# Sums of x in a two-layer kernel: their places in the passes moved, the first groups loaded ahead, the second layer's first buffers swapped

## The chip, the cores and the metric

The kernel runs on one core of one Trainium2 chip. The metric is device time in microseconds (us), the median of several executions. Three executions of the kernel before took 1288.52, 1289.45 and 1290.34 us. TensorE (PE) multiplies, its weight loads (PEld) run beside it; ScalarE (ACT), VectorE (DVE) and GpSimd (POOL) work element by element, and SyncE (SP) hands out nearly all DMAs, in the order in which they stand on its queue.

## The reference, cut to what matters

```python
# attention: q, k, v of (8, 8, 576, 64)
scores = scale * np.matmul(q, k.transpose(0, 1, 3, 2))
thresh = np.max(scores, axis=-1, keepdims=True) - tau
scores = np.where(scores >= thresh, scores, -1e9)
attn = softmax(scores)                      # written out in the reference
attn_out = np.matmul(attn, v)
x = attn_out.transpose(0, 2, 1, 3).reshape(4608, 512)
# two layers
h = np.maximum(x @ w_in, 0.0)               # (4608, 512) @ (512, 2048)
out = h * h @ w_out                         # (4608, 2048) @ (2048, 512)
```

All of it is float32. The change concerns the two layers after the attention.

## The kernel before, in words

**Stages.** The attention writes x transposed to DRAM (`xT`, one tensor for each of the 8 batches). The first layer begins at 496 us of the profiled execution and goes to 889 us, the second from there to the end. Both are multiplied by a scheme of Strassen's kind, applied twice (an outer and an inner level): instead of 8 x 8 = 64 block products it makes 7 x 7 = 49, and pays for that with sums of blocks ahead of the products and behind them. The seven operands of a level are called 1 to 7. Four of them (1, 7, 2, 3 for x) are the blocks themselves; 5, 6, 4 and a new 7 are sums: `SUMS_B` says 5 = 7 - 1, 6 = 3 - 5, 4 = 2 - 6, 7 = 3 - 7, in this order, the last one in place.

**Passes and products.** The first layer has nine passes, 0 to 8 (`PASSES`). They work on six sets of x (`SETS`), of 512 or 1024 columns: set 0 in pass 0, set 1 in passes 1 and 2, set 2 in 3 and 4, set 3 in 5 and 6, set 4 in pass 7 and set 5 in pass 8. Each of the two passes of a wide set has half of the outputs. A pass has 49 products, 0 to 48: seven groups, one for each outer operand m in the order 1, 2, 6, 7, 4, 5, 3 (`OUTER`), and in each group seven products for the inner operands in the order 1, 6, 7, 5, 2, 4, 3. A product fills one PSUM bank of 512 columns. A wide product is two matmuls of 256 columns, a narrow one four of 128; in the trace each matmul leaves two records.

**A group** (`inner`, L729 to L761) uses four banks, X, Y, Z, W, of six in a ring. X is copied to SBUF by ACT (`p1`, L764), Y and Z are taken out by DVE with a sum (`u2`, `u3`, L128), W by DVE with a sum; then three more products are added into X, Z and W, each of which needs the bank to have been read, and are taken out as well. In group 1 the last X is a copy by ACT (L951). `final` (L947) adds the results up, on DVE where nothing else is added and else as a DVE sum into a ring of six places `t` and a POOL addition (L128 on POOL) that reads the place. Groups 2, 4, 5 and 3 give outputs `o`.

**Squares.** Each output is squared by ACT in two instructions (`square`, L905 and L906) and stored by SP (L909). `squares_due(6)` at the end of each product's `tick` takes one from the list when it is five products old. So the squares of group 3, made in products 45 to 48, stand on ACT's queue in products 1 to 4 of the next pass, behind those of group 5 (products 43 to 46).

**Sums of x.** While two passes run on one set, the sums of the next set are made by ACT and DVE together: `sum_v` (L855) lets ACT copy one operand to a PSUM place `c` (L868; two such places) and returns the DVE operation that subtracts it (L125). `plan` (L1189) says for each set what is loaded and summed at which product, counted from the beginning of two passes: `loads` issue DMAs from `xT` (`load_set`, L828), `work` makes sums. `sum_outer` makes a whole outer operand from raw ones, in chunk 0 (inner 1 and 7) or 1 (inner 2 and 3); `sum_inner` makes one inner operand for one or more outer ones at once, if their places lie at even distances. The copy of a sum is issued at its product, and `finish_sum` (L1197), called at every product, issues the DVE operation at the next one. The places of the sets in SBUF (`PLACES`, `AT[4]`) are chosen so that a group of the next set comes into a place that a group of the set before has left; a load waits for that.

**Beside these** POOL makes sums of the second layer's weights in small steps (`chain_out`, L1168): SP loads four blocks from DRAM (L1180), POOL makes four subtractions (L125 on POOL), SP stores the results (L1185). In pass 7 the sums of set 5 are made by `prepare_x`, one step at a product (L1254). In the last pass the first sums for the second layer are made.

**The second layer** (`output_layer`, L1043) has nine passes of narrow products (L1074) on the stored squares. It has the same groups; its places come from rings `fin` (L994 to L998), among them `t` for p1, u2 and u3. At each product `also` (L1287) does part of the list of sums (`work_of`, `spread`) and, while any is left from the first layer, a square. Place 13 * 512, the first of ring `t`, is the last of the four places that pass 8 keeps for U2 and that POOL reads at its end.

The order of all of this is written out by hand (`manual_schedule`): each engine's queue holds its instructions in the order in which the program issues them.

## Time and profile before

| what | value |
|---|---|
| median of 3 executions | 1289.45 us |
| the profiled execution | 1290.65 us |
| its span, first to last instruction | 1288.8 us |
| mean granted TensorE clock in it | 0.997 |
| first layer's products in the span | 496.2 to 889.0 us |
| second layer's products | from 889.1 us |

One execution is profiled. A row of a timeline has the start in us from the beginning of the span, the length in us, engine, line, operation, written and read names, sizes and the count of merged instructions; in brackets stands how long the engine stood idle before it and who ended that. A row of the groups or the issues has count and then mean or median; a row of the waits has total us, times and the longest. Lines are those of the kernel before.

### The profile page before, as it was taken

Reading aid. Unit: us, or ns where it says so; the run is one execution under the profiler, and the core shown is the slowest. Engines: PE = TensorE matmul, PEld = TensorE weight load, DVE = VectorE, ACT = ScalarE, POOL = GpSimd, SP = SyncE. Lnnn points to the kernel's source line nnn. Section 1 sums busy time; section 2 is a strip of 40 time slices with the busy share of each in tenths; the row PEclk is TensorE's granted clock in tenths of the full one; section 3 lists DMA queues with packets and bytes.
Section 4 is the critical chain, followed back from the end, with each engine's and each line's share of the span. In section 5 each row is a group of like instructions: output and inputs, shape, how many; then the busy total and the mean of one; then the engine's idle time right before and its main releaser. Section 6 shows DMA issues by size and latency. Waiting matters only on the chain. (4 is left out here: it accounts for less than half of the span.)

```text
span 1288.8 us, 44113 instructions
## 1 busy us (share of the span) xinstructions
PE 1259.3 (98%) x17451; PEld 1090.0 (85%) x17451; DVE 998.9 (78%) x2437; ACT 852.9 (66%) x1540; POOL 897.4 (70%) x1094
## 2 busy tenths in 40 slices
PE   8999999999999999999999999999999999999998
PEld 5666666677777769988888888999999999999998
DVE  6999999999999997887778777877745664665463
ACT  6999999999999994655765766666523432343240
POOL 2565656655555556887797788768777867776775
PEclk9999999999999999999999999999999999999999
DMA  5555666544333423457567556589545314522411
GB/s 143 147 160 145 164 195 189 142 95 112 90 81 88 101 46 99 158 160 218 181 196 213 175 180 190 184 316 393 193 147 164 109 61 160 164 80 89 160 34 34
DMA packets 256590, 191.88 MB, mean 149 GB/s; under 512 B 96000, under 2 KB 217344, under 8 KB 256384
## 3 DMA queue, kind: packets, MB, share of 16 engines
q1 hardware_dynamic: 254928, 188.63, 49.1%
q8 instruction: 137, 2.24, 0.7%
q14 instruction: 69, 0.57, 0.1%
q10 hardware_dynamic: 1456, 0.44, 0.1%
HBM read 116.65 MB, written 72.35 MB: 147 GB/s over the span
## 5 line engine op out<-in xcount | busy, mean ns | idle before, releaser
L128 POOL TENSOR_TENSOR arena<-arena 128x512 f32<-128x512 f32 (+1 forms) x314 | 377.9, 1222 | 130.3 <-DVE arena L128 117.3
L1074 PE MATMUL po<-wall,arena 128*128 128x128 f32 x3528 | 394.7, 275 | 1.4 <-ACT arena L764 1.4
L1074 PEld LDWEIGHTS po<-wall,arena 128*128 128x128 f32 x3528 | 394.2, 192 | 1.8 <-ACT arena L764 1.8
L935 PE MATMUL ph<-arena,wall 128*128 128x128 f32 (+1 forms) x2352 | 389.4, 328 | 4.1 <-DVE arena L128 3.3
L935 PEld LDWEIGHTS ph<-arena,wall 128*128 128x128 f32 x2352 | 353.8, 191 | 39.6 <-DVE arena L128 7.9
L128 DVE TENSOR_TENSOR arena<-ph,arena 128x512 f32<-128x512 f32 x378 | 253.8, 687 | 71.9 <-PE ph L935 43.5
L125 POOL TENSOR_TENSOR arena<-arena 128x128 f32<-128x128 f32 (+2 forms) x314 | 255.3, 814 | 31.8 <-DMA arena<-w 13.8
L128 DVE TENSOR_TENSOR arena<-po,arena 128x128 f32<-128x128 f32 x378 | 108.2, 289 | 168.7 <-PE po L1074 164.5
L469 ACT ACTIVATE arena<-arena 128x576 f32<-128x576 f32 x288 | 227.7, 885 | 16.2 <-DVE arena L459 16.2
L474 DVE SCALAR_TENSOR_TENSOR arena<-arena 128x576 f32<-128x576 f32 x288 | 225.6, 812 | 0.5 <-POOL arena L466 0.5
L459 DVE TENSOR_SCALAR_CACHE_REDUCE arena<-sc 128x576 f32<-128x576 f32 x288 | 204.4, 750 | 15.6 <-ACT arena L531 6.4
L868 ACT COPY c<-arena 128x512 f32<-128x512 f32 (+3 forms) x307 | 173.9, 573 | 62.7 <-DVE arena L125 54.1
L125 DVE TENSOR_TENSOR arena<-arena,c 128x512 f32<-128x512 f32 (+3 forms) x271 | 175.3, 655 | 18.6 <-ACT c L868 15.8
L540 PEld LDWEIGHTS sc<-arena 64*64 64x64 f32 x5760 | 146.0, 134 | 42.4 <-DVE arena L459 38.9
L441 PE MATMUL sc<-arena 64*64 64x64 f32 (+1 forms) x2304 | 170.9, 417 | 0.4 <-DVE arena L661 0.4
L540 PE MATMUL sc<-arena 64*64 64x128 f32 (+1 forms) x5760 | 162.1, 263 | 8.4 <-DVE arena L459 6.2
L531 ACT COPY arena<-pt 128x1024 f32<-128x1024 f32 x144 | 161.2, 1119 | 3.7 <-PE pt L384 3.7
L764 ACT COPY arena<-po 128x128 f32<-128x128 f32 x63 | 16.6, 264 | 186.8 <-PE po L1074 184.0
L384 PEld LDWEIGHTS pt<-ident,arena 64*128 64x128 f32 x2304 | 83.0, 139 | 43.1 <-ACT arena L531 36.0
L764 ACT COPY arena<-ph 128x512 f32<-128x512 f32 x63 | 36.6, 581 | 104.7 <-PE ph L935 104.6
L384 PE MATMUL pt<-ident,arena 64*128 64x64 f32 x2304 | 100.7, 227 | 4.0 <-ACT arena L531 3.8
L441 PEld LDWEIGHTS sc<-arena 64*64 64x64 f32 x2304 | 64.1, 133 | 47.0 <-issue 22.2
(51 smaller groups left out, 952.2 us busy)
## 6 DMA issues: line engine op xcount, KB each, us to landing
g<-arena SPq DMA_DIRECT2D x144, 256.0 KB, 2.6
arena<-g SPq DMA_DIRECT2D x144, 256.0 KB, 5.0
w<-arena SPq DMA_DIRECT2D x60, 256.0 KB, 2.5
wall<-w SPq DMA_DIRECT2D x49, 256.0 KB, 5.2
arena<-w SPq DMA_DIRECT2D x44, 256.0 KB, 3.4
arena<-in_v_dram SPq DMA_DIRECT2D x32, 288.0 KB, 3.8
out_dram<-arena SPq DMA_DIRECT2D x70, 128.0 KB, 2.2
arena<-in_q_dram SPq DMA_DIRECT2D x64, 128.0 KB, 4.0
```

The source lines that it names most:

```text
L125: e.tensor_tensor(out=out, in0=x, in1=y, op=ALU.subtract)
L128: e.tensor_tensor(out=out, in0=x, in1=y, op=ALU.add)
L384: made = nc.tensor.transpose(pt[:, r, ts(slot, HALF)], of[rows, :], ident[rows, rows])
L441: made = nc.tensor.matmul(sc[at, ds(to, count)], lhs, kT[rows, ds(at_k, count)], start=True, stop=True)
L459: made = nc.vector.tensor_scalar(out=s[:, j, :], in0=sc[:, ds(at, S)], scalar1=1.0, scalar2=None, op0=ALU.mult, op1=ALU.min, accum_out=nmx ...
L469: nc.scalar.activation(out=w[:, :, j, :], in_=of(j), func=AF.Exp, bias=nmx[:, j : j + 1], scale=-1.0)
L474: nc.vector.scalar_tensor_tensor(out=w[:, :, j, :], in0=of(j), scalar=thr[:, j : j + 1], in1=w[:, :, j, :], op0=ALU.is_le, op1=ALU.mult, a ...
L531: touch("weights", nc.scalar.copy(joined(to), whole(pt, 0, count)), at, 2 * BANK, m)
L540: made = nc.tensor.matmul(sc[ds(u * D, D), ds(5 * j * BANK + row, count)], loaded_v[i][rows, (c - (u != j)) % CH, :], wT[m][rows, ds(weigh ...
L868: nc.scalar.copy(c, y)
L935: nc.tensor.matmul(to[:, j, :], W_IN[m, k][:, ts(h * parts_ + j, P)], x_of(m, k), start=(not more and j == 0), stop=True, skip_group_check ...
L1074: nc.tensor.matmul(to, g[:, j, :], w[:, j, :], start=(not more and j == 0), stop=(j == 3), skip_group_check=True)
```

## The change

The change moves work and adds none to PE.

- `finish_sum` and `summed`: the DVE operation of a sum is issued two products behind its copy (or with the next sum's copy, if that comes earlier), not one.
- The plans of sets 1 to 4 are written anew. No sum stands in the last products of a pass or the first five of the next one; in between they stand closer, mostly two products apart. Inner sums of group 2 are made early and alone, those of 6 with 7 and of 4 with 5 in pairs, those of 3 alone.
- Loads: group 1 of sets 2 and 3 (and 1 and 7 of set 4) is loaded 14 products before the two passes begin. Group 2 is loaded at product 21 and group 3 at 28, where it was the other way round. Set 4's second load goes from product 14 to 7.
- `PLACES` and `AT[4]` follow from that. Inner operand 7 of group 2 is no longer made in place but at a place of its own (`ASIDE`), as outer sum 4 still reads the raw one later.
- Pass 7: the steps of `prepare_x` stand in products 17 to 40 without a pause, not in the first six of each seven from product 14.
- Second layer: the two halves of ring `t` change their order; the four outer sums of its first group are put ahead of the sum for inner operand 7 of group 2; what is left of the squares goes at the second and third product of a group, not at the last two.

```diff
@@ places
-        1: {7: 0, 1: 1, 2: 2, 3: 3, 5: 4, 6: 5, 4: 6},
-        2: {1: 7, 7: 1, 5: 2, 3: 5, 2: 0, 6: 6, 4: 4},
-        3: {1: 3, 7: 7, 5: 0, 3: 6, 2: 1, 6: 4, 4: 2},
+        1: {1: 0, 7: 1, 2: 2, 3: 3, 5: 4, 6: 5, 4: 6},
+        2: {1: 7, 7: 0, 5: 2, 2: 5, 3: 1, 6: 6, 4: 4},
+        3: {1: 3, 7: 7, 5: 5, 2: 6, 3: 0, 6: 4, 4: 2},
...
+        if w > NQ and (m, k) == (2, 7):
+            return arena[:, ds(ASIDE, w)]
@@ rings of the second layer
-    fin.ring("t", [13 * BANK + P * i for i in range(4)] + [XI + 2 * BANK + P * i for i in range(4)])
+    fin.ring("t", [XI + 2 * BANK + P * i for i in range(4)] + [13 * BANK + P * i for i in range(4)])
@@ the plans
-        def finish_sum():
-            while open_sum:
-                open_sum.popleft()()
+        def finish_sum(wait=2):
+            while open_sum and open_sum[0][0] + wait <= clock["n"]:
+                open_sum.popleft()[1]()
...
         tail = {
-            57: (out_, 4, 1), 60: (in_, (7, 4), 5), 63: (in_, (7, 4), 6), 66: (in_, (7, 4), 7), 69: (in_, (7, 4), 4),
-            72: (in_, (5, 3), 5), 75: (in_, (5, 3), 6), 78: (in_, (5, 3), 7), 81: (in_, (5, 3), 4),
+            54: (out_, 4, 0), 56: (in_, (6, 7), 5), 58: (in_, (6, 7), 6), 60: (in_, (6, 7), 7), 62: (in_, (6, 7), 4), 65: (out_, 4, 1),
+            68: (in_, (4, 5), 5), 70: (in_, (4, 5), 6), 72: (in_, (4, 5), 7), 74: (in_, (4, 5), 4),
+            78: (in_, (3,), 5), 81: (in_, (3,), 6), 83: (in_, (3,), 7), 85: (in_, (3,), 4),
         }
         plan(1, 0, {0: (7, 1, 3, 2)}, {
-            9: (out_, 5, 0), 12: (out_, 5, 1), 15: (in_, (1,), 5), 18: (in_, (1,), 6), 21: (in_, (1,), 4), 24: (out_, 6, 0),
-            27: (out_, 6, 1), 30: (out_, 7, 0), 33: (out_, 7, 1), 36: (in_, (1,), 7), 39: (out_, 4, 0),
-            42: (in_, (2, 6), 5), 45: (in_, (2, 6), 6), 48: (in_, (2, 6), 7), 52: (in_, (2, 6), 4), **tail,
+            10: (in_, (1,), 5), 12: (in_, (1,), 6), 14: (in_, (1,), 4), 16: (out_, 5, 0), 19: (out_, 5, 1), 21: (in_, (1,), 7),
+            23: (out_, 6, 0), 26: (out_, 6, 1), 29: (out_, 7, 0), 31: (out_, 7, 1),
+            34: (in_, (2,), 5), 36: (in_, (2,), 6), 38: (in_, (2,), 7), 40: (in_, (2,), 4), **tail,
         })
         for i in (2, 3):
-            plan(i, (2 * i - 2) * 49, {0: (1,), 7: (7,), 21: (3,), 28: (2,)}, {
-                6: (in_, (1,), 5), 9: (in_, (1,), 6), 12: (in_, (1,), 4), 15: (out_, 5, 0), 18: (out_, 5, 1), 21: (in_, (1,), 7),
-                27: (out_, 7, 0), 30: (out_, 7, 1), 36: (out_, 6, 0), 39: (out_, 6, 1), 43: (out_, 4, 0),
-                46: (in_, (2, 6), 5), 48: (in_, (2, 6), 6), 51: (in_, (2, 6), 7), 54: (in_, (2, 6), 4), **tail,
+            plan(i, (2 * i - 2) * 49, {-14: (1,), 7: (7,), 21: (2,), 28: (3,)}, {
+                8: (in_, (1,), 5), 10: (in_, (1,), 6), 12: (in_, (1,), 4), 15: (out_, 5, 0), 18: (out_, 5, 1), 21: (in_, (1,), 7),
+                27: (in_, (2,), 5), 29: (in_, (2,), 6), 31: (in_, (2,), 7), 33: (in_, (2,), 4),
+                35: (out_, 6, 0), 37: (out_, 7, 0), 39: (out_, 6, 1), 41: (out_, 7, 1), **tail,
             })
         four = (1, 7, 2, 3)
-        plan(4, 6 * 49, {7: (1, 7), 14: (3, 2)}, {
-            22: (out_, 5), 25: (out_, 7), 28: (in_, four, 5), 31: (in_, four, 6), 34: (in_, four, 4), 37: (out_, 6), 40: (out_, 4),
-            43: (in_, four, 7), 46: (in_, (6, 4), 5), 49: (in_, (6, 4), 6), 52: (in_, (6, 4), 7), 55: (in_, (6, 4), 4),
-            58: (in_, (5,), 5), 61: (in_, (5,), 6), 64: (in_, (5,), 7), 67: (in_, (5,), 4),
+        plan(4, 6 * 49, {-14: (1, 7), 7: (3, 2)}, {
+            22: (out_, 5), 24: (out_, 7), 27: (in_, four, 5), 29: (in_, four, 6), 31: (in_, four, 4), 35: (out_, 6), 38: (out_, 4),
+            41: (in_, four, 7), 54: (in_, (6, 4), 5), 56: (in_, (6, 4), 6), 58: (in_, (6, 4), 7), 60: (in_, (6, 4), 4),
+            62: (in_, (5,), 5), 63: (in_, (5,), 6), 64: (in_, (5,), 7), 65: (in_, (5,), 4),
         })
@@ pass 7, and the second layer's lists
-                if before_last and 2 <= i <= 5 and at < 6:
+                if before_last and 17 <= tick < 41:
                     next(xsums)
...
-                    work += outer_sums(0, 6, (1, 2)) + outer_sums(0, 5, (4,)) + outer_sums(0, 6, (4,))
+                    work[3:3] = outer_sums(0, 6, (1, 2)) + outer_sums(0, 5, (4,)) + outer_sums(0, 6, (4,))
...
-                if at > 4:
+                if at in (1, 2):
                     squares_due(0)
```

More of the change, by code (lines that the diff above doesn't have):

```diff
@@ L783 @@
     AT[4] = {}
-    for m, s_, e in ((1, 3, 0), (7, 3, 1), (2, 1, 0), (3, 1, 1), (5, 4, 0), (6, 2, 0), (4, 2, 1)):
+    for m, s_, e in ((1, 1, 0), (7, 1, 1), (2, 3, 0), (3, 3, 1), (5, 4, 0), (6, 2, 0), (4, 2, 1)):
         AT[4][m] = SPOT[s_] + GROUP * e
@@ L836, in sum_inner @@
         op, x, y = next((op, x, y) for op, z, x, y in SUMS_B if z == o)
+        if ms == (2,) and o == 7:
+            return add(op, x_block(i, 2, 7), x_blocks(i, ms, x), x_blocks(i, ms, y))
         return add(op, x_blocks(i, ms, o), x_blocks(i, ms, x), x_blocks(i, ms, y))
@@ L969, in final @@
                     row, col = {2: (0, 0), 4: (1, 0), 5: (1, 1), 3: (0, 1)}[m]
-                    squares.append((clock["n"], s, 4 * (2 * row + ab[0]) + 2 * col + ab[1], o))
+                    squares.append((clock["n"] , s, 4 * (2 * row + ab[0]) + 2 * col + ab[1], o))
             def tick(at):
```

9 lines of the change are left out of this document (5 added, 4 removed).

## The prediction

> **What bounds the kernel now.** I read the page first, then the timelines of PE and of its weight loads, then those of ACT, DVE, SP and POOL around the places where PE stops. Passes 0 to 8 are those of the first layer, products 0 to 48 the steps of a pass; a wide product is four records, a narrow one (passes 0, 7, 8 and the second layer) eight.
>
> ```profile
> span 1288.8 us, 44113 instructions
> PE 1259.3 (98%) x17451; PEld 1090.0 (85%) x17451; DVE 998.9 (78%) x2437; ACT 852.9 (66%) x1540; POOL 897.4 (70%) x1094
> ```
>
> PE is busy almost throughout; the change leaves its records as they are. It can only take away the moments in which PE waits. The timeline of PE merges records that follow each other and starts a new row where it waited:
>
> ```profile
> 593.90 36.53 PE L935 MATMUL ph<-arena,wall 128*128 128x256 f32 x168 [0.47 <-DVE arena L128]
> 630.75 6.52 PE L935 MATMUL ph<-arena,wall 128*128 128x256 f32 x28 [0.33 <-DVE arena L128]
> 637.77 79.30 PE L935 MATMUL ph<-arena,wall 128*128 128x256 f32 x364 [0.50 <-DVE arena L128]
> 717.56 6.52 PE L935 MATMUL ph<-arena,wall 128*128 128x256 f32 x28 [0.49 <-DVE arena L128]
> 724.58 79.74 PE L935 MATMUL ph<-arena,wall 128*128 128x256 f32 x384 [0.50 <-DVE arena L128]
> 805.07 6.52 PE L935 MATMUL ph<-arena,wall 128*128 128x128 f32 x56 [0.75 <-DVE arena L128]
> 811.88 18.39 PE L935 MATMUL ph<-arena,wall 128*128 128x128 f32 x160 [0.29 <-DVE arena L128]
> ...
> 889.07 3.74 PE L1074 MATMUL po<-wall,arena 128*128 128x128 f32 x32
> 893.36 12.83 PE L1074 MATMUL po<-wall,arena 128*128 128x128 f32 x112 [0.56 <-ACT arena L764]
> 907.05 378.14 PE L1074 MATMUL po<-wall,arena 128*128 128x128 f32 x3384 [0.86 <-ACT arena L764]
> ```
>
> The first record of the first layer stands in the view of its line, and the weight loads have a stretch without a wait:
>
> ```profile
> L935 PE MATMUL ph<-arena,wall x2352: 273/378/483, 496.2 to 889.0; 128*128 128x128 f32 x98, 128*128 128x256 f32 x98
> ```
> ```profile
> 645.04 70.66 PEld L935 LDWEIGHTS ph<-arena,wall 128*128 128x128 f32 x328 [0.16 <-DVE arena L128]
> ```
>
> 70.66/328 = 0.2154 us for a wide record, 378.14/3384 = 0.1117 for a narrow one; a wide product is 0.862 us, a narrow one 0.894. Counted out between the row starts, the lost time is:
>
> - start (496.2) to 593.90, product 12 of pass 2: 392 narrow and 244 wide records are 96.4 us, 97.65 passed: **1.3** lost.
> - to 637.77, product 12 of pass 3: 196 wide, 42.2 of 43.87: **1.65**.
> - to 724.58, product 12 of pass 5: 392 wide, 84.4 of 86.81: **2.4**.
> - to 811.88, product 12 of pass 7: 344 wide, 96 narrow, 84.8 of 87.30: **2.5**.
> - to 889.07: 688 narrow, 76.9 of 77.19: **0.3**.
> - the second layer to 907.05: 144 narrow, 16.1 of 17.98: **1.9**. From there on nothing.
>
> Together 10.0 us. That is all the change can win: it doesn't touch the attention part.
>
> The losses stand at the starts of passes 3, 5 and 7, and the reason is read on ACT and DVE at the start of pass 5:
>
> ```profile
> 713.60 0.63 ACT L905 ACTIVATE arena<-arena 128x512 f32<-128x512 f32 x1 [0.69 <-POOL arena L128]
> ...
> 714.79 0.58 ACT L868 COPY c<-arena 128x512 f32<-128x512 f32 x1
> ...
> 716.06 0.63 ACT L905 ACTIVATE arena<-arena 128x512 f32<-128x512 f32 x1 [0.17 <-POOL arena L128]
> ...
> 717.26 0.58 ACT L868 COPY c<-arena 128x512 f32<-128x512 f32 x1
> 717.77 0.62 ACT L905 ACTIVATE arena<-arena 128x512 f32<-128x512 f32 x1
> ...
> 720.14 0.57 ACT L951 COPY arena<-ph 128x512 f32<-128x512 f32 x1
> 720.61 0.63 ACT L905 ACTIVATE arena<-arena 128x512 f32<-128x512 f32 x1
> ...
> 721.81 0.58 ACT L868 COPY c<-arena 128x512 f32<-128x512 f32 x1
> 722.32 0.58 ACT L764 COPY arena<-ph 128x512 f32<-128x512 f32 x1
> ```
> ```profile
> 712.37 0.69 DVE L128 TENSOR_TENSOR arena<-ph,arena 128x512 f32<-128x512 f32 x1 [0.65 <-POOL arena L128]
> 712.97 0.68 DVE L125 TENSOR_TENSOR arena<-arena,c 128x512 f32<-128x512 f32 x1
> 714.83 0.69 DVE L128 TENSOR_TENSOR arena<-ph,arena 128x512 f32<-128x512 f32 x1 [1.17 <-POOL arena L128]
> ...
> 722.42 0.69 DVE L125 TENSOR_TENSOR arena<-arena,c 128x512 f32<-128x512 f32 x1 [2.13 <-ACT c L868]
> 723.02 1.51 DVE L128 TENSOR_TENSOR arena<-ph,arena 128x512 f32<-128x512 f32 x2
> ```
>
> ACT still has the squares of the pass before (L905 with L906, 1.2 us from start to start), some held by POOL, and copies for sums of x between them. So p1 of group 2 (L764, 722.32) is late, DVE waits 2.13 for a copy, and the eviction that frees product 12's bank (second of the two at 723.02) ends at 724.53: PE starts at 724.58.
>
> **The change part by part.**
>
> *No sums of x around a start, copies two products ahead* (L1187 to L1226). The built kernel's instruction order has no copy c from product 42 of a pass to product 4 of the next; the copy after the eight squares is at product 5, and p1 of group 2 stands behind it, as now. Of the copies above, that at 714.79 lies in the wait for POOL that ends at 716.06, so taking it away wins nothing; only the one at 717.26 stands on the path. Without it: square to 717.26, two more to 719.64, L951 to 720.11, the last square to 721.31, copy, p1 at 721.82 instead of 722.32: **0.5** at pass 5. Pass 3 is built alike: **0.5**. At pass 7 the copy on the path is a small one:
>
> ```profile
> 806.18 0.36 ACT L868 COPY c<-arena 128x256 f32<-128x256 f32 x1
> ```
>
> and wins its 0.30 (the next square starts at 806.48): **0.3**. What is late next is POOL, then the eight squares. A comparison shows it: pass 4 starts without a sum and without a stall.
>
> ```profile
> 671.30 0.69 DVE L128 TENSOR_TENSOR arena<-ph,arena 128x512 f32<-128x512 f32 x1 [1.02 <-POOL arena L128]
> ```
> ```profile
> 677.76 0.37 ACT L868 COPY c<-arena 128x256 f32<-128x256 f32 x1
> ```
>
> There the squares are over at 677.76, in pass 5 at 721.81: 44.05 later, a dense pass being 42.2. So pass 5 is 1.8 us later within itself, and the change takes 0.5 of that. DVE's wait for POOL (671.30, 714.83) is 43.53 apart, 1.3 of the 1.8, and POOL's work isn't changed; it is late because of its own waits:
>
> ```profile
> POOL arena L125 <- DMA arena<-w: 13.8, 10, 4.5
> ```
>
> *Group 1 loaded 14 products ahead.* Before, the load stands at product 0 and the copy at product 6 of pass 2 waits for it:
>
> ```profile
> 591.35 0.38 ACT L868 COPY c<-arena 128x256 f32<-128x256 f32 x1 [1.10 <-DMA arena<-xT]
> ```
>
> With it goes most of the 1.3 lost up to 593.90: **1.2**. The load's two DMAs now stand on SP ahead of four squares' stores; nothing near waits for these.
>
> *Groups 2 and 3 change places; group 2's inner sums come early.* The copy at product 27 of passes 2 and 4 now reads group 2, loaded at product 21:
>
> ```profile
> 604.20 1.18 SPq L828 DMA_DIRECT2D arena<-xT  x2
> ```
> ```profile
> arena<-xT SPq DMA_DIRECT2D x14, 256.0 KB, 3.3
> arena<-xT SPq DMA_DIRECT2D x4, 384.0 KB, 5.6
> ```
>
> The second issue is at about 604.8; by the two rows it lands between 608.1 and 610.4. Product 27 ends at 593.90 + 64 x 0.2154 = 607.7, so ACT waits 0.4 to 2.7. Behind this copy on ACT is p1 of product 28, behind that DVE's u2; PE needs p1 at product 32, 611.1, and copy and p1 take 0.9. Cost 0 to 0.2; I take 0. The Trainium skill (DMA: Bandwidth & Descriptors, Anatomy of one DMA) gives a DMA about 2.0 us and its bytes at 436 GB/s; as an estimate from that page the load would land at 607.4 and no copy would wait. The rows here are longer, and the rows decide.
>
> *Sums of 512 closer together.* In products 7 to 13 of passes 1, 3, 5 stand four sums and six evictions. At DVE's 0.60 from start to start (712.37, 712.97) that is 6.0 us of 6.03. A sum slips in front of an eviction by 0.6 at most, and PE asks for a bank three products after it filled it, some 0.8 us after the eviction in time. Cost 0 to 0.5 each; I take 0, because the groups ahead of and behind these hold two sums at most and DVE starts the seven products on time. Four copies between group 4's squares (products 35 to 41 of passes 2 and 4: 4 x 0.51 + 4 x 1.2 + 0.48 = 7.3 us in 6.03) make p1 at product 42 late by 1.3 and cost up to 0.5, but the stall before product 12 of the next pass is set by POOL and ACT, not by when PE arrives, and swallows it.
>
> *Pass 7's sums* (L1257) start three products later, behind the squares of group 2: of the 0.3 lost there, **0.25**.
>
> *The second layer's first places* (L996, L1276, L1298).
>
> ```profile
> 893.04 0.27 ACT L764 COPY arena<-po 128x128 f32<-128x128 f32 x1 [2.77 <-POOL arena L128]
> ...
> 906.75 0.25 ACT L764 COPY arena<-po 128x128 f32<-128x128 f32 x1
> ```
>
> The first p1 writes a place that POOL still reads; ACT stood 2.77 us. In its new place it can go at 890.3. The two squares move from products 5, 6 to 1, 2 and fill just this time; the other two from 12, 13 to 8, 9, so they are done before p1 at product 14 (now 906.75, just ahead of 907.05). ACT's work in products 7 to 13, seven copies, two squares and a p1, is 3.6 + 2.4 + 0.2 = 6.2 us of 6.26. Both stalls go. DVE's sum for operand 7 of group 2 now comes last, at product 6, needed by product 9: 0 to 0.3 lost. Of 1.9: **1.7**.
>
> Sum: 0.5 + 0.5 + 0.3 + 1.2 + 0.25 + 1.7 = 4.45. The profiled execution took 1290.65 (span 1288.8 and 1.85 around it), 1.2 over the median of 1289.45. 1290.65 - 4.45 = 1286.2; on the median **1285.0**.
>
> **The rivals.**
>
> *A: POOL isn't what holds the starts.* If squares start as early as at pass 4 once the sums are gone, all 10.0 us go: 1279.5. For it: pass 4, with the same eight squares, has no stall. Against it: the 1.3 us by which DVE's wait for POOL ends later.
>
> *B: new waits take the place.* DVE's full groups slip 0.5 at three passes, the late p1 of product 42 isn't swallowed (2 x 0.5), the first places win half (0.9 less): 3.4 lost, 1288.4. For it: 6.0 of 6.03 leaves no room.
>
> *C, slower: SP hands out the load of group 2 late.* SP issues in order, and a store that waits for a square holds all behind it:
>
> ```profile
> 586.30 4.52 SPq L909 DMA_DIRECT2D g<-arena  x4
> ```
>
> Issued 4.5 us later at product 21, as here at the start of pass 2, the load lands at 612.6 to 614.9 where PE can spare it until 610.2: PE stops for 2.4 to 4.7 us, in passes 2 and 4, and the same hold meets group 3's load at product 28, first read at 37, for about as much again. That is 10 to 19 lost; at 10, 1295. It decides as soon as the landing passes 610.2. Against it: SP has four stores at this place today too and issued at 604.20, 1.6 after product 21's end. The Trainium skill (DMA: Bandwidth & Descriptors, Anatomy of one DMA) says that a wait is held by the issuing sequencer before dispatch, which is this mechanism; the row above agrees.
>
> **How the numbers follow.** Forecast 0.58, its own range 1283.3 to 1286.8 (the unknown costs above, and 1 us on the good side); A 0.20, with halves of it 1279.5 to 1283.3; B 0.14; C 0.08. That the sums aren't moved as said has no chance: the order of the built kernel shows them moved. A measurement tells about 0.2% from no change: 1286.9 and 1292.0 are the bounds. Forecast and A are faster: 0.78; B the same: 0.14; C slower: 0.08. For 8 in 10 the range takes the forecast, most of A and half of B: 1280.5 to 1287.8.
>
> **What would show it.** In the changed timeline of PE: no row start in pass 2, nor in the second layer behind its first; one stop of about 1 us near product 12 of passes 3 and 5, and two in pass 7. On ACT at pass 5, the square that waits for POOL at 716.06 in the same distance to its pass, and p1 0.5 earlier. Wrong would be: PE rows through passes 3 to 7 without a stop (A), stops in products 8 to 13 with DVE never waiting (B), or ACT's copy of product 27 ended by a DMA with PE stopping behind it (C).

## The result, and the profile after

The changed kernel takes 1286.80 us in the median of 22 executions, the kernel before 1289.89 on the same chips: a ratio of 0.9972, 95% interval 0.9961 to 0.9983, or 3.6 us less (2.2 to 5.0). The ratio is that of the means (1287.12 and 1290.72), so it isn't quite that of the medians. Forecast were 1285.0 us, 4.45 less, with a range of 1280.5 to 1287.8. The profiled execution has a span of 1284.0 us, 4.8 shorter than that of before; over the 22 executions it is 3.6, so a part of these 4.8 may be the difference of two single executions. Page of the kernel after:

```profile
span 1284.0 us, 44140 instructions
...
PE 1256.2 (98%) x17451; PEld 1087.8 (85%) x17451; DVE 1000.5 (78%) x2449; ACT 856.3 (67%) x1552; POOL 895.2 (70%) x1094
```

PE has as many records as before; DVE and ACT have 12 more each, as some sums that were made for two operands at once are now made alone. Where the gain stands is shown by two stretches: the first layer, and the first pass of the second. Columns are the length and the busy time (and count) of PE, PEld, DVE, ACT and POOL, then PE's clock, DMA share and GB/s. First the kernel before, then after:

```profile
496.25:889.07 392.82, 389.22 (x2353) 353.85 (x2354) 304.16 (x482) 251.26 (x458) 326.31 (x378) 1.00 0.64 204
889.07:934.85 45.78, 44.36 (x395) 43.98 (x393) 31.93 (x76) 26.02 (x51) 34.95 (x30) 1.00 0.71 251
```
```profile
496.19:885.78 389.59, 388.20 (x2353) 353.82 (x2353) 305.47 (x494) 254.51 (x470) 325.70 (x378) 1.00 0.65 206
885.78:930.02 44.24, 44.03 (x394) 43.84 (x393) 31.73 (x76) 26.21 (x51) 34.90 (x30) 1.00 0.72 260
```

392.82 to 389.59 is 3.2 us won in the first layer, 45.78 to 44.24 is 1.5 in the second; ahead of both nothing moved (496.25 and 496.19). So the size is near what was forecast. The places are not. Where the first layer still waits is read on PE's weight loads of the kernel after, whose rows begin anew at each stop:

```profile
618.52 5.05 PEld L941 LDWEIGHTS ph<-arena,wall 128*128 128x128 f32 x24 [0.47 <-DVE arena L128]
624.08 11.95 PEld L941 LDWEIGHTS ph<-arena,wall 128*128 128x128 f32 x56 [0.51 <-DVE arena L128]
636.58 0.73 PEld L941 LDWEIGHTS ph<-arena,wall 128*128 128x128 f32 x4 [0.55 <-DVE arena L128]
637.77 2.46 PEld L941 LDWEIGHTS ph<-arena,wall 128*128 128x128 f32 x12 [0.47 <-DVE arena L128]
640.82 68.93 PEld L941 LDWEIGHTS ph<-arena,wall 128*128 128x128 f32 x320 [0.59 <-PE ph L941]
710.61 12.82 PEld L941 LDWEIGHTS ph<-arena,wall 128*128 128x128 f32 x60 [0.86 <-DVE arena L128]
723.90 2.46 PEld L941 LDWEIGHTS ph<-arena,wall 128*128 128x128 f32 x12 [0.47 <-DVE arena L128]
726.95 68.93 PEld L941 LDWEIGHTS ph<-arena,wall 128*128 128x128 f32 x320 [0.59 <-PE ph L941]
```

618.52 and 624.08 are products 41 and 47 of pass 2, 710.61 product 47 of pass 4: stops that the kernel before didn't have. 636.58 is product 12 of pass 3; 637.77 and 723.90 are product 13, 640.82 and 726.95 product 16 of passes 3 and 5. Behind 726.95 no start of a pass has a stop. In the timeline of PE, the second layer after:

```profile
885.78 8.20 PE L1080 MATMUL po<-wall,arena 128*128 128x128 f32 x72
894.19 386.18 PE L1080 MATMUL po<-wall,arena 128*128 128x128 f32 x3456 [0.21 <-DVE arena L125]
```

The two stops are gone, and there is a new one of 0.47 before product 9, ended by a DVE sum.

Here, and in all that follows, a stop is the time from the start of a PE record to the next start, less 0.216 us (wide) or 0.112 (narrow), counted where more than 0.02 is left. "Start" is products 0 to 13 of a pass; the others are products 14 to 20 of passes 1, 3 and 5, and 30 to 35 and 40 to 48 of passes 0, 2, 4 and 6. Every row is one profiled execution, in us; the names are those of the runs below. One execution need not be a typical one: that of a_load14 took 1290.29 us, where its median is 1286.02. And the ratios to before of all a_ and v_ kernels but v_spread overlap with that of the kernel after, so the experiments are read by their stops.

| kernel | start 2 | start 3 | start 5 | start 7 | 14-20 | 30-35 | 40-48 | second layer | rest | sum |
|---|---|---|---|---|---|---|---|---|---|---|
| before | 1.08 | 1.91 | 2.17 | 1.64 | 0.02 | 0 | 0.35 | 2.01 | 0.49 | 9.67 |
| b_nosum | 0.58 | 1.77 | 1.36 | 1.03 | 0 | 0.44 | 0.29 | 2.18 | 0.34 | 7.99 |
| b_nopool | 0 | 1.09 | 1.09 | 0 | 0.03 | 0.37 | 0 | 2.00 | 0.48 | 5.06 |
| b_early | 0.73 | 2.26 | 2.63 | 1.67 | 0 | 0.04 | 0.04 | 2.00 | 0.49 | 9.87 |
| b_nosum_early | 0 | 1.08 | 1.31 | 0.66 | 0 | 0.10 | 0 | 2.09 | 0.34 | 5.58 |
| b_places | 0.18 | 2.80 | 2.17 | 1.14 | 0.02 | 0.91 | 0 | 0 | 0.49 | 7.70 |
| after | 0 | 0.74 | 0.33 | 0 | 1.11 | 0.06 | 1.94 | 0.47 | 0.25 | 4.91 |
| a_nocopy6 | 0 | 1.55 | 1.15 | 0 | 1.10 | 0.76 | 0.49 | 0.47 | 0.54 | 6.06 |
| a_wait1 | 0 | 1.05 | 1.29 | 0 | 0 | 0.81 | 0.90 | 0.47 | 0.26 | 4.78 |
| a_load14 | 0 | 0.75 | 1.24 | 0 | 1.10 | 1.81 | 1.94 | 0.47 | 0.26 | 7.57 |
| a_loads | 0 | 0.56 | 0.57 | 0 | 1.10 | 0.55 | 1.94 | 0.47 | 0.26 | 5.45 |
| v_spread | 0 | 0 | 0.47 | 0 | 4.41 | 0.15 | 2.04 | 0.47 | 4.06 | 11.60 |
| v_near | 0 | 0.62 | 0.63 | 0 | 1.38 | 0 | 4.87 | 0 | 0.84 | 8.33 |
| v_last | 0 | 0.74 | 0.57 | 0 | 1.12 | 0 | 2.01 | 0 | 0.27 | 4.71 |

4.76 less from before to after: the starts of 3, 5 and 7 gave 4.65 (forecast 1.3), pass 2's start 1.08 (1.2), the second layer 1.54 (1.7), and products 14 to 20 and 40 to 48 took 2.7 back (forecast nothing). Two errors of the forecast cancel, and that is luck.

Why the starts gave so much is read at pass 5, on ACT, DVE and POOL of the kernel after, and last on POOL of the kernel before:

```profile
714.70 0.63 ACT L911 ACTIVATE arena<-arena 128x512 f32<-128x512 f32 x1 [0.60 <-POOL arena L128]
...
719.93 0.58 ACT L874 COPY c<-arena 128x512 f32<-128x512 f32 x1
720.44 0.58 ACT L764 COPY arena<-ph 128x512 f32<-128x512 f32 x1
```
```profile
713.46 0.69 DVE L128 TENSOR_TENSOR arena<-ph,arena 128x512 f32<-128x512 f32 x1 [0.88 <-POOL arena L128]
```
```profile
710.92 6.21 POOL L128 TENSOR_TENSOR arena<-arena 128x512 f32<-128x512 f32 x5
```
```profile
711.05 7.44 POOL L128 TENSOR_TENSOR arena<-arena 128x512 f32<-128x512 f32 x6
```

Pass 5 begins at 712.48 before and at 712.45 after. POOL's additions end at 718.49 before, 6.01 into the pass, and at 717.13 after, 4.68. The square that waits for POOL goes at 714.70 instead of 716.06. POOL has the same work and is 1.3 us less behind: the forecast had said that this lag would stay. A part of this stands in pass 4, where POOL waits for a chain's load, before and then after:

```profile
699.95 0.46 POOL L125 TENSOR_TENSOR arena<-arena 128x128 f32<-128x128 f32 x1 [1.61 <-DMA arena<-w]
```
```profile
698.61 0.45 POOL L125 TENSOR_TENSOR arena<-arena 128x128 f32<-128x128 f32 x1 [1.07 <-DMA arena<-w]
```

Pass 4 begins at 670.18 and 669.42, so this wait ends 29.8 and 29.2 us into it, and POOL's additions end 48.3 and 47.7 us after its beginning: 0.6 of the 1.3. The other 0.7 is that pass 5 itself begins 0.7 later (43.03 us after pass 4, not 42.30). Just ahead of it, in product 44 of pass 4, stand a copy, p1 of the group and the DVE operation that waits for it:

```profile
707.55 0.58 ACT L874 COPY c<-arena 128x512 f32<-128x512 f32 x1
708.06 0.58 ACT L764 COPY arena<-ph 128x512 f32<-128x512 f32 x1
```
```profile
708.67 0.69 DVE L128 TENSOR_TENSOR arena<-ph,arena 128x512 f32<-128x512 f32 x1 [0.78 <-ACT arena L764]
```

From there comes the new stop of 0.72 at product 47. The theory after the result was: while PE stands there, POOL and ACT catch up, so part of the stop is only moved; the rest of the gain is the sums' own. Rivals: the sums alone held the starts; or POOL alone did; or loads that the change moved on SP.

### The profile page after: what moved, and what is told of

Same layout as the page of the kernel before. It is cut to its first block, busy times and chain, and to the rows that moved or that the text cites. A ratio compares the mean times of both kernels' runs of the same rounds, so it can differ in the third digit from the quotient of the medians.

```text
span 1284.0 us, 44140 instructions
## 1 busy us (share of the span) xinstructions
PE 1256.2 (98%) x17451; PEld 1087.8 (85%) x17451; DVE 1000.5 (78%) x2449; ACT 856.3 (67%) x1552; POOL 895.2 (70%) x1094
## 4 chain that ended last, share of the span: by engine, by line
PE 61%; DVE 2%; DMA 2%; ACT 2%; issue 1%; SPq 0%; POOL 0%; DVEq 0%; ACTq 0%; POOLq 0%
PE po L1080 30%; PE ph L941 26%; PE sc L540 2%; PE sc L441 2%; DMA wall<-w 1%; DVE arena L128 1%; PE pt L384 1%; ACT arena L911 1%; ACT c L874 0%; DMA g<-arena 0%; DVE arena L125 0%; PE sc L384 0%; PE sc L402 0%; DVE arena L459 0%; ACT arena L764 0%
## 5 line engine op out<-in xcount | busy, mean ns | idle before, releaser
L125 POOL TENSOR_TENSOR arena<-arena 128x128 f32<-128x128 f32 (+2 forms) x314 | 254.7, 812 | 29.8 <-DMA arena<-w 10.6
L874 ACT COPY c<-arena 128x512 f32<-128x512 f32 (+2 forms) x319 | 176.0, 558 | 105.8 <-DVE arena L125 86.6
L469 ACT ACTIVATE arena<-arena 128x576 f32<-128x576 f32 x288 | 220.8, 834 | 16.2 <-DVE arena L459 16.2
L125 DVE TENSOR_TENSOR arena<-arena,c 128x512 f32<-128x512 f32 (+2 forms) x283 | 176.9, 634 | 9.9 <-ACT c L874 8.2
L531 ACT COPY arena<-pt 128x1024 f32<-128x1024 f32 x144 | 154.0, 1070 | 4.3 <-PE pt L384 4.3
L466 POOL TENSOR_SCALAR arena<-arena,tau_p 128x2 f32<-128x2 f32 x144 | 65.2, 453 | 45.8 <-DVE arena L459 39.1
```

The costliest lines, as they stand in the source:

```text
L125: e.tensor_tensor(out=out, in0=x, in1=y, op=ALU.subtract)
L469: nc.scalar.activation(out=w[:, :, j, :], in_=of(j), func=AF.Exp, bias=nmx[:, j : j + 1], scale=-1.0)
L531: touch("weights", nc.scalar.copy(joined(to), whole(pt, 0, count)), at, 2 * BANK, m)
L874: nc.scalar.copy(c, y)
```

## The experiments

Names with b_ are edits of the kernel before, with a_ and v_ of the kernel after.

**b_nosum** leaves the sums around the starts out.

```diff
-            42: (in_, (2, 6), 5), 45: (in_, (2, 6), 6), 48: (in_, (2, 6), 7), 52: (in_, (2, 6), 4), **tail,
+            **tail,
...
-                46: (in_, (2, 6), 5), 48: (in_, (2, 6), 6), 51: (in_, (2, 6), 7), 54: (in_, (2, 6), 4), **tail,
+                **tail,
...
-            43: (in_, four, 7), 46: (in_, (6, 4), 5), 49: (in_, (6, 4), 6), 52: (in_, (6, 4), 7), 55: (in_, (6, 4), 4),
+            43: (in_, four, 7),
```

> The kernel before, with the sums whose copies stand from product 42 of a pass to product 6 of the next left out (inner sums of 2 and 6 in sets 1 to 3, of 6 and 4 in set 4; the kernel then multiplies blocks that weren't summed, and nothing else of it changes). Forecast's reading (a sum is worth only the copy of 0.5 or 0.3 us that lies on ACT's path, POOL's lag stays): PE's stops in products 0 to 13 shrink from 1.9, 2.2 and 1.6 us in passes 3, 5 and 7 to 1.4, 1.7 and 1.3, in all 1.3 less. Rival (the sums alone hold the starts): the three go to under 0.4 each, some 5 us less in all, without a new stop in products 41 to 48. Third reading (the stop was moved to products 44 to 47 by the change): as the forecast's, since nothing holds PE there in this kernel.

Its timeline of PE, and POOL at the start of its pass 5 (which begins at 711.33):

```profile
592.47 18.40 PE L935 MATMUL ph<-arena,wall 128*128 128x256 f32 x84 [0.31 <-DVE arena L128]
...
630.33 85.48 PE L935 MATMUL ph<-arena,wall 128*128 128x256 f32 x392 [0.65 <-DVE arena L128]
716.30 86.00 PE L935 MATMUL ph<-arena,wall 128*128 128x256 f32 x412 [0.48 <-DVE arena L128]
802.92 83.68 PE L935 MATMUL ph<-arena,wall 128*128 128x128 f32 x744 [0.62 <-DVE arena L128]
```
```profile
708.92 8.68 POOL L128 TENSOR_TENSOR arena<-arena 128x512 f32<-128x512 f32 x7
```

Each start still has its stop; the three together fell from 5.72 to 4.16, by 1.6 (0.1, 0.8 and 0.6). POOL's additions end at 717.60, 6.27 into the pass, as late as before. The rival "sums alone" falls. In this pair the forecast's 1.3 for the sums was about right; by all five executions of the table with these starts (5.7, 6.6 and 6.1 with the sums, 4.2 and 3.1 without) it is rather 2.5. Ratio to before 0.9956 (0.9937 to 0.9976).

**b_nopool** keeps the chains' DMAs and drops their arithmetic.

```diff
-                    minus(nc.gpsimd, t[:, to, :], t[:, x, :], t[:, y, :])
+                    pass
```

> The kernel before, with POOL's four subtractions of each of the 49 chains for the second layer's weights left out (their loads and stores stay; those weight sums are then not computed). Forecast's reading (POOL's lag is 1.3 of the 1.8 us by which pass 5 starts late, the copy 0.5): stops in products 0 to 13 of passes 3, 5 and 7 shrink from 5.7 us together to about 1.5. Rival (the sums alone): they stay above 4.5. If either cause is enough by itself: they stay near 5.7 here and in the kernel without the sums.

```profile
633.01 85.64 PE L935 MATMUL ph<-arena,wall 128*128 128x256 f32 x392 [0.45 <-DVE arena L128]
719.11 162.65 PE L935 MATMUL ph<-arena,wall 128*128 128x256 f32 x1128 [0.46 <-DVE arena L128]
```

These are the only two rows of the first layer that begin anew behind pass 2's start. The three starts come to 2.18, the forecast's reading with 0.7 more than it gave; pass 2's stop is gone as well, with its load where it was. Ratio 0.9964 (0.9945 to 0.9982). So POOL's lag and the copies add up: neither is the whole.

**a_nocopy6** asks whether the new stop at product 47 is what freed the starts.

```diff
-                35: (out_, 6, 0), 37: (out_, 7, 0), 39: (out_, 6, 1), 41: (out_, 7, 1), **tail,
+                **tail,
```

> The kernel after, with the four sums at products 35 to 41 of passes 2 and 4 left out (outer sums 6 and 7 of sets 2 and 3, which are then not computed). PE's stops in products 41 to 47 of these passes are 0.72 each in the kernel after. Reading 'moved' (that stop is what gave POOL the time): they go, and the stops at the starts of passes 3 and 5 grow by 0.5 to 0.7 each; the sum of all stops stays near 4.9. Reading 'added' (the stop is a cost of its own beside starts that are free now): they go, the starts stay as they are, the sum is about 3.5.

Weight loads around the starts of passes 3 and 5, and POOL at the start of pass 5 (714.49):

```profile
632.48 5.05 PEld L941 LDWEIGHTS ph<-arena,wall 128*128 128x128 f32 x24 [0.53 <-DVE arena L128]
...
639.35 0.73 PEld L941 LDWEIGHTS ph<-arena,wall 128*128 128x128 f32 x4 [0.90 <-DVE arena L128]
...
725.57 0.73 PEld L941 LDWEIGHTS ph<-arena,wall 128*128 128x128 f32 x4 [0.91 <-DVE arena L128]
```
```profile
712.55 7.45 POOL L128 TENSOR_TENSOR arena<-arena 128x512 f32<-128x512 f32 x6
```

The stops of products 41 to 47 went, 1.45 in all, and the starts of passes 3 and 5 grew from 1.07 to 2.70, by 1.63. POOL ends 5.5 into pass 5, not 4.7. That is the reading "moved". It is clear in pass 3 (1.55, against 0.56 to 0.75 in four executions with the same code up to there but for copies in passes 2 and 4 of one: after, a_load14, a_loads, v_last); pass 5's 1.15 lies among the 0.33 to 1.24 of these four. Against their means the two starts grew by 1.3. The sum is 6.06 and not 4.9 because a load came later (0.70 in products 30 to 35) and pass 7 has 0.28 more. Ratio 0.9967 (0.9951 to 0.9982).

How the three quantities hang together, at the start of pass 5 (us from the pass's first record; POOL's additions end, p1 of group 2 starts, PE is late at product 12):

| kernel | POOL ends | p1 | late |
|---|---|---|---|
| before, pass 4 | 4.79 | 7.88 | 0.02 |
| after | 4.68 | 8.00 | 0.02 |
| b_nopool | 3.88 | 8.75 | 0.67 |
| a_nocopy6 | 5.52 | 8.81 | 0.74 |
| b_nosum | 6.27 | 9.06 | 0.94 |
| before | 6.01 | 9.84 | 1.76 |

PE is on time while p1 starts by 8.0; each 0.1 later costs about 0.1. p1 follows POOL's end by 2.8 without a copy among the squares (b_nosum), by 3.3 with one (after, a_nocopy6), by 3.8 with two (before). In b_nopool, 4.9 behind, POOL no longer sets it.

**a_wait1** undoes the distance of two products alone.

```diff
-        def finish_sum(wait=2):
+        def finish_sum(wait=1):
```

> The kernel after, with the DVE operation of a sum issued one product behind its copy, as in the kernel before, and all else as in the kernel after. Forecast's reading (the places of the copies matter, not the distance): the sum of all stops stays within 0.5 us of 4.9. Rival (the second product is what keeps DVE from waiting behind a late copy at a start): stops in products 4 to 13 of passes 3, 5 and 7 come back, 0.5 us or more in each.

```profile
637.66 85.54 PE L941 MATMUL ph<-arena,wall 128*128 128x256 f32 x392 [0.78 <-DVE arena L128]
724.08 76.19 PE L941 MATMUL ph<-arena,wall 128*128 128x256 f32 x359 [0.87 <-DVE arena L128]
```

The sum stays (4.78), but both readings have a part: products 14 to 20 lose their 1.11, products 40 to 48 half of their 1.94, and the starts of 3 and 5 get 1.27 more. So the stop at product 16 isn't made by a full DVE alone, as the forecast feared: DVE works without a pause there in both kernels (in the kernel after from 720.54 to past product 16 of pass 5, in a_wait1 from 635.12 past that of pass 3). What differs is the order: an operand (inner 7 of 6 and 7, copied at product 11), whose sum is issued two products behind its copy and so behind more evictions, comes too late for product 16, which reads it. In the kernel after, pass 5, the sum ends at 726.84 and PE goes on at 726.98. In passes 3 and 5 of a_wait1 PE also comes to product 16 later, behind longer stops at product 12. Pass 1, where nothing stops PE in products 0 to 15 of either kernel, shows the order alone: 0.18 at product 16, and 0 in a_wait1. Ratio 0.9954 (0.9935 to 0.9974).

**a_load14 and a_loads** put set 4's loads back, the second alone and then both.

```diff
-        plan(4, 6 * 49, {-14: (1, 7), 7: (3, 2)}, {
+        plan(4, 6 * 49, {-14: (1, 7), 14: (3, 2)}, {      (a_load14)
+        plan(4, 6 * 49, {7: (1, 7), 14: (3, 2)}, {        (a_loads)
```

> The kernel after, with set 4's second load (outer operands 3 and 2, three issues on SP) at product 14 of pass 6, where the kernel before has it, and not at product 7. Reading 'queue' (in the kernel before these three issues, 1.5 us, stand on SP ahead of the stores and of the chain's store at product 16, so the chain's next loads go out 2 us later and POOL waits 1.9 us for one of them): POOL's wait for arena<-w in products 33 to 36 of pass 6 comes back, 1 to 2 us, its additions end near 6 instead of 4.6 us into pass 7, and PE stops 0.5 to 1.5 us in products 4 to 12 of pass 7, where it has no stop now. Rival (pass 7's start is free because no sum of x stands around it, whatever SP's order): no stop there, the sum of all stops stays near 4.9.

> The kernel after, with both loads of set 4 at the products of the kernel before (7 and 14 of pass 6, not 35 of pass 5 and 7 of pass 6). With the second one alone at 14 (the run before this) pass 7 started without a stop. Reading 'two loads' (in the kernel before the first load slows the chain's store that is issued right behind it, and by that the second load lands on the next store, 4.3 us from its issue to the next chain load instead of 2.5; POOL falls 2 us behind): POOL waits over 1 us for arena<-w in products 28 to 36 of pass 6, ends its additions past 6 us in pass 7, and PE stops there again, 0.3 to 1.2 us. Rival (the loads don't matter; sums of x in pass 6 did it): no stop in pass 7.

Both miss: pass 7 starts without a stop in either, so the loads alone are not what freed it (ratios 0.9961, 0.9943 to 0.9979, and 0.9963, 0.9947 to 0.9979). What differs is the chain's store at product 25 or 26 of pass 6 and the load behind it. SP's queue before, then in a_loads, and POOL before:

```profile
779.62 0.53 SPq L1185 DMA_DIRECT2D w<-arena  x1
784.79 0.36 SPq L1180 DMA_DIRECT2D arena<-w  x1
```
```profile
778.55 0.53 SPq L1191 DMA_DIRECT2D w<-arena  x1
781.88 0.36 SPq L1186 DMA_DIRECT2D arena<-w  x1
```
```profile
787.72 0.46 POOL L125 TENSOR_TENSOR arena<-arena 128x128 f32<-128x128 f32 x1 [1.90 <-DMA arena<-w]
```

The load goes out when the store has landed: 5.2 us later in the one, 3.3 in the other, and POOL then waits 1.90 or 0.11. Before and in b_nosum, b_nosum_early, b_places and b_nopool this store took 4.3 to 5.1 us; in a_load14, a_nocopy6, a_wait1 and v_near 2.5 to 2.7. SP's queue shows what goes with it: in all kernels of before this store follows a chain's load and a square's store by 1.0 to 1.3 and 0.6 to 0.8 us, in the kernel after (and its edits but a_loads) the chain's load by 2.8 to 3.2. In a_loads the distance is 1.1 again, as the chain's store ahead takes 4.2 us beside set 4's loads (2.3 in a_load14), and yet the store shown took less than in any kernel of before. Which edit makes that so stays open.

**b_early** moves one load in the kernel before.

```diff
-            plan(i, (2 * i - 2) * 49, {0: (1,), 7: (7,), 21: (3,), 28: (2,)}, {
+            plan(i, (2 * i - 2) * 49, {-14: (1,), 7: (7,), 21: (3,), 28: (2,)}, {
```

> The kernel before, with the load of group 1 of sets 2 and 3 14 products ahead of the two passes and nothing else changed. Forecast: the copy at product 6 of pass 2 no longer waits for a DMA (1.10 us before), and the stop before product 12 of pass 2 goes, 1.1 us. Rival (that start is held by POOL, as the kernel without POOL's subtractions has no stop there with the load where it was): half a us or more stays.

ACT at the start of pass 2:

```profile
588.25 0.63 ACT L906 ACTIVATE arena<-arena 128x512 f32<-128x512 f32 x1
588.78 0.37 ACT L868 COPY c<-arena 128x256 f32<-128x256 f32 x1
```

The copy follows the last square and waits for no DMA any more, yet 0.73 of the 1.08 stays; the rival is right. POOL's additions end 5.66 into pass 2 here and 4.81 before. Ratio 0.9985 (0.9964 to 1.0005), not to be told from no change.

**b_nosum_early** has both edits.

> The kernel before without the sums around the starts (as in the run that left them out) and with group 1 of sets 2 and 3 loaded 14 products ahead. Pass 2's start had a stop of 1.08 us in the kernel before, 0.58 without the sums, 0.73 with the early load. Reading 'both': with both edits the stop goes, under 0.1, as in the kernel after, and the starts of passes 3, 5 and 7 stay at 3.5 to 4.7 us together. Rival (POOL's lag holds pass 2 too): 0.3 or more stays in pass 2.

Pass 2's stop goes, 1.08 to 0; the starts of 3, 5 and 7 come to 3.05, lower than expected. Ratio 0.9972 (0.9957 to 0.9987). But that pass 2 needed both edits isn't shown: none of the sums left out stands at its start (52 of set 1's plan is product 3 of pass 1). The traces say what differs:

| kernel | load | copy of product 6 starts, us into pass 2 | held by | POOL ends | stop |
|---|---|---|---|---|---|
| before | product 0 | 8.80 | the load | 4.81 | 1.08 |
| b_nosum | product 0 | 8.28 | the load | 4.90 | 0.58 |
| b_places | product 0 | 7.89 | the load | 4.84 | 0.18 |
| b_nopool | product 0 | 7.58 | the load | 3.60 | 0 |
| b_early | early | 8.44 | the squares | 5.66 | 0.73 |
| b_nosum_early | early | 7.63 | the squares | 4.84 | 0 |

With the load at product 0 the stop is as long as the load is late, and that varies. With the load early the squares set it, and so POOL: in pass 1 of b_early it waited 0.83 for chains' loads, in before and b_nosum_early for none. So the early load frees pass 2 where POOL is on time, and why POOL was late in b_early stays open.

**b_places** has two of the second layer's three edits.

```diff
-    fin.ring("t", [13 * BANK + P * i for i in range(4)] + [XI + 2 * BANK + P * i for i in range(4)])
+    fin.ring("t", [XI + 2 * BANK + P * i for i in range(4)] + [13 * BANK + P * i for i in range(4)])
...
-                if at > 4:
+                if at in (1, 2):
```

> The kernel before, with the two halves of the second layer's ring t exchanged and its squares at the second and third product of a group, and the list of its first sums as it was. Forecast: the stops before products 4 and 18 of the second layer's first pass (0.8 and 1.1 us) go. The kernel after has a stop of 0.47 before product 9; if the new order of the sums is its cause, there is none here, and the second layer wins 1.9 to 2.0. If the squares at products 8 and 9 are its cause, it is here too and 1.5 are won.

```profile
890.76 394.12 PE L1074 MATMUL po<-wall,arena 128*128 128x128 f32 x3528
```

The second layer is one row, all 2.0 won. The third edit, the list's order, is what costs 0.47 at product 9. Ratio 0.9988 (0.9968 to 1.0008), not to be told from no change.

**v_spread, v_near, v_last** try to win what is left.

```diff
(v_spread: second of two passes)
+            57: (in_, (6, 7), 5), 59: (in_, (6, 7), 6), 61: (in_, (6, 7), 7), 64: (in_, (6, 7), 4), 66: (out_, 4, 0), 68: (out_, 4, 1),
+            71: (in_, (4, 5), 5), 73: (in_, (4, 5), 6), 75: (in_, (4, 5), 7), 78: (in_, (4, 5), 4),
...
(v_near: wait=1, old order of the second layer's list, and)
+            56: (out_, 4, 0), 57: (in_, (6, 7), 5), 59: (in_, (6, 7), 6), 61: (in_, (6, 7), 7), 63: (in_, (6, 7), 4), 66: (out_, 4, 1),
...
+                28: (in_, (2,), 5), 29: (in_, (2,), 6), 31: (in_, (2,), 7), 33: (in_, (2,), 4),
+                34: (out_, 6, 0), 36: (out_, 7, 0), 38: (out_, 6, 1), 40: (out_, 7, 1), **tail,
(v_last: old order of the list, and)
+                28: (in_, (2,), 5), 30: (in_, (2,), 6), 31: (in_, (2,), 7), 33: (in_, (2,), 4),
```

> The kernel after, with the sums of sets 1 to 3 in the second of two passes begun at product 8 instead of 5 and three of them in each seven products instead of four, and those of products 35 to 41 of the first of the two passes one product earlier. If late copies and a full DVE in products 7 to 13 make the stops there: the stops in products 12 to 16 of passes 3 and 5 (1.2 and 0.8 us in the kernel after) go, those of products 41 to 47 shrink a little, and the sum of all stops falls from 4.9 to 2 to 3 us. If POOL makes them: the sum stays above 4.

v_spread makes outer sum 4 behind the in-place sum 7 that it reads, so from a block that is already overwritten. Its weight loads in pass 3:

```profile
650.16 8.50 PEld L941 LDWEIGHTS ph<-arena,wall 128*128 128x128 f32 x40 [0.97 <-DVE arena L125]
...
663.52 54.26 PEld L941 LDWEIGHTS ph<-arena,wall 128*128 128x128 f32 x252 [0.97 <-DVE arena L125]
```

Start 3 is free, but products 19 and 33 wait 0.84 each for a sum, in three passes: their copies stand four products ahead of the product that reads them (15 and 19, 29 and 33), in the kernel after six and eight. Sum of stops 11.60, ratio 1.0018 (0.9999 to 1.0037). The expectation failed.

> The kernel after with the DVE operation one product behind its copy, the sums of the second of two passes begun at product 7 behind the group's own copy, the copy that waits for group 2's load one product later (behind p1 of the group), sums of products 35 to 41 one earlier, and the second layer's first list in the order of the kernel before. From the rows so far: the 0.47 at the second layer's product 9 goes (as in the kernel with the places alone), the 0.06 to 0.8 at products 32 to 34 goes, the copy of 0.5 ahead of group 2's p1 goes and with it the stops at product 12 of passes 3 and 5, unless the four sums behind it fill DVE and stop PE in products 13 to 16 (0.8 each). Sum of all stops 1.5 to 3.5, against 4.9 in the kernel after; rival (POOL's lag sets the starts whatever the copies do): 4 or more.

DVE and PE of v_near in pass 2:

```profile
614.31 0.69 DVE L125 TENSOR_TENSOR arena<-arena,c 128x512 f32<-128x512 f32 x1 [3.64 <-DMA arena<-xT]
```
```profile
616.45 22.80 PE L941 MATMUL ph<-arena,wall 128*128 128x256 f32 x100 [2.72 <-DVE arena L128]
```

Here the prediction's rival C is seen: a DVE sum brought two products nearer to group 3's load waits 3.64 for it, holds the evictions behind it, and PE stops 3.3. SP hands that load out at 607.65, product 33 and not 28, behind a chain's load that goes out when a chain's store has landed (601.42 to 606.49); in the kernel after it is product 33 too (611.42), but there DVE asks later and waits 0.59. The expectation failed too: the sum is 8.33, ratio 0.9979 (0.9966 to 0.9992).

> The kernel after with two edits: the second layer's first list in the order of the kernel before (the kernel with the places alone had no stop at product 9), and the copies for the inner sums 5 and 6 of group 2 of sets 2 and 3 at products 28 and 30 instead of 27 and 29, so that p1 of product 28 stands ahead of the copy that waits for the load. The DVE operation stays two products behind (in the run with one product, a sum of DVE waited 3.6 us for group 3's load and PE stopped 3.3). Expected: the stop of 0.47 before product 9 of the second layer and those of products 32 and 33 of pass 2 (0.06 to 1.6 in the runs of this family) go, the others stay: 3.9 to 4.6 in all. Rival (the copy moved behind p1 only shifts the wait into products 35 to 41, which are full): stops there grow by as much as is won.

```profile
888.93 394.12 PE L1080 MATMUL po<-wall,arena 128*128 128x128 f32 x3528
```

The stop at product 9 and those of products 30 to 35 are gone; 4.71, since its starts have 0.24 and products 40 to 48 0.07 more than the kernel after. Ratio to before 0.9963 (0.9945 to 0.9981): better than before, and not to be told from the kernel after (0.9961 to 0.9983).

## Why the prediction was right, and where it wasn't

- **What bounds the kernel** held: PE's stops, 9.7 us, of which 4.8 went, all of it outside the attention.
- **The sum** came out by luck in part: the starts of 3, 5 and 7 won 3.35 more than forecast, and new stops that were taken as 0 cost 2.7.
- **No sums around a start, 0.5 + 0.5 + 0.3.** Mis-sized: 4.65 went. The step that failed is "POOL's work isn't changed", by which 1.3 of pass 5's 1.8 us would stay: its work isn't changed, but its lag is (4.68 us into pass 5, not 6.01). The sums alone are worth 1.6 to 2.5 (b_nosum). In passes 3 and 5 some 1.3 to 1.6 was moved to products 41 to 47 (a_nocopy6). In pass 7 POOL's wait of 1.90 for a chain's load is gone, by a shorter store; the moved loads alone don't explain that, and its cause stays open.
- **Group 1 loaded ahead, 1.2.** 1.08 went. But b_places, with pass 2 as before, had 0.18 there, and b_early, with the load ahead, had 0.73, as POOL was late: the stop that was priced varies from run to run, with the landing of the load and with POOL's lag, and the forecast counted only the first.
- **Groups 2 and 3 exchanged, 0 to 0.2.** The copy waited until 608.68, inside the 608.1 to 610.4 of the forecast, and PE lost 0.06. In other executions of the same order 0.15 to 1.81 was lost in products 30 to 35 (0 to 0.91 with the old order): the range was too narrow, and the cover almost nil. The load's two DMAs took 4.2 and 4.6 us. So the estimate of 607.4, which the prediction worked out from the Trainium skill (DMA: Bandwidth & Descriptors, Anatomy of one DMA), was too early; that section has its figures from DMAs that GpSimd issues, and SP issues these.
- **Sums closer together, taken as 0.** Products 14 to 20 cost 1.1, with sums two products behind their copies in a DVE that has no pause there; with one product it is 0, and the starts cost more (a_wait1). The late p1 behind four copies and squares cost 1.44 in passes 2 and 4; most of it is swallowed by the next start (a_nocopy6), as the forecast said.
- **Pass 7's sums, 0.25.** The stop at product 26 went from 0.26 to 0.18: 0.08.
- **Second layer, 1.7.** 1.54; both old stops went, the new order of the list costs 0.47, where 0 to 0.3 was allowed.
- **The signs.** One stop near product 12 of pass 3 is there (0.41, and 0.33 at product 13); pass 5 has 0.33 at product 13 alone and pass 7 none, where two were to stay. Passes 2 and 4 and the second layer have new stops. The square that waits for POOL was to keep its distance from the beginning of pass 5 and comes 1.3 earlier, p1 1.8 earlier and not 0.5.
- **Rivals.** A (POOL isn't what holds the starts) falls by b_nopool. B's mechanism came with 2.7 us in the first layer and 0.5 in the second, against its 3.4, beside a larger gain. C's came at the sizes above, not at 10.

## What to carry to other kernels

A stop behind a chain of engines is not removed until every engine in the chain has caught up; if a new stop appears earlier, put it back alone (as a_nocopy6 does) before booking the gain. A sum has two ends: its copy must not stand ahead of an urgent instruction, and its result must be there before its reader; four products were too few here, five too few with the DVE operation two products behind, six enough. And where effects are 1 us in 1290, count the stops in one stage; do not compare spans.

## What the runs showed of the hardware that wasn't expected

- **The same code gives other stops.** Pass 5's start had 0.33, 0.57, 1.24 and 0.57 us in four executions whose instructions up to there are the same but for copies in passes 2 and 4 of one (after, a_loads, a_load14, v_last); the first layer began between 492.3 and 499.6 us in the 14 profiled executions, with nothing changed ahead of it. Effects under about 1 us at one place need more than one profile.
- **An instruction packet beside a late store.** DMA in the kernel before from 781.5 to 784.5 us (GB/s in 40 slices; queue, packets, MB, share of 16 engines), then in a_loads from 780.43 to 782.83, both from 1.88 us after the issue of the chain's store:

```profile
GB/s 301 314 300 300 273 294 519 314 232 219 130 48 21 0 0 0 0 0 14 0 14 14 14 0 14 14 14 14 20 20 20 27 20 20 20 20 20 14 0 0
...
q8 instruction: 1, 0.02, 1.9%
```
```profile
GB/s 350 324 324 316 290 324 316 324 324 333 214 205 94 85 333 51 17 0 0 0 0 0 0 0 0 0 0 0 0 0 0 0 0 0 0 0 0 0 0 0
...
q8 instruction: 1, 0.02, 2.4%
```

Before, the bulk has passed after 1 us, and then 14 to 27 GB/s trickle for 1.5 us until 784.3: about a sixteenth of the 300 of the bulk, one engine's part. One packet of 0.02 MB of the instruction queue falls into the stretch, 1.9% of 16 engines times 3 us, 0.9 us: from 781.98 to 782.91, where the trickle begins. In a_loads it falls so late that nothing is left behind it. That the packet holds up one engine's share of the store is argued from these rows; no run tested it, and it isn't what makes most stores late: of 98 chains' stores in the 14 traces that took over 4 us, 50 had no such packet from 1 us before their issue to their landing. The Trainium skill (Runtime: NRT & Kernel Launch, Instruction fetch mechanics) says that instructions are fetched in blocks of 16 KiB over a DMA queue, and (DMA: Bandwidth & Descriptors, Queues, rings and completion order) that an engine takes turns between its queues packet by packet; the size (16384 bytes in the trace) agrees with the first, and the place where the trickle begins fits the second.
